# Announcing a loop's jump back in every pass except the last

## The chip, the cores and the metric

One core of a Trainium2 chip. The metric is the device time of one execution in microseconds (us), lower is better. Of each kernel several executions were timed and one was traced; "the trace" is that one.

## The reference

One decode step: layer norm of a single token, attention of 16 heads, each over its own cache of 65,536 keys and values of 256 numbers, an output projection, and a gated dense branch beside it. What matters is the cache: 1.07 GB of bf16 are read once.

```python
x = A_x
xn = _layernorm(x, axis=-1)
s = _A_ref(xn, A_k_cache, A_v_cache, A_wq, A_wo)   # scores, softmax, weighted values, @ wo
g = _silu(_B_ref(xn, B_w1, B_w2))
return x + s * g
```

## The kernel before

The cache is cut into 64 blocks of 8 MB of keys and 8 MB of values. Three buffers of 8 MB hold, in turn, the keys of a block and then the values of the same block. VectorE multiplies the keys with the query and sums most products, ScalarE sums the rest and makes the softmax, TensorE finds the row maximum and multiplies with the values, and SyncE's queue issues the transfers. Each engine has its own loop of three blocks a pass, synchronised by semaphores alone.

```python
    def load_k(i, s):
        take(sp, vf[s])                 # the values in this buffer are used up
        sp.dma_start(out=R[s][:, :], in_=block(Kd, i)).then_inc(kl[s], 16)
        sp.sem_inc(kh[s], 16)

    def load_v(i, s):
        take(sp, kf[s])                 # the keys in this buffer are used up
        sp.dma_start(out=R[s][:, :], in_=block(Vd, i)).then_inc(vl[s], 16)

    def pe_v(s):
        take(pe, pv)
        take(pe, vl[s], 16)
        pe_keys(psO, s, s, 0, KB, True, True, od)      # 64 matmuls
        pe_mark().then_inc(vf[s], 1)

    def pe_block(i, s):
        pe_turn()
        pe_max(i)
        pe_v(s)

    def loop(e, a, b, step, **kw):
        return nc.Fori(a, b, step, engines={e}, head_slot={e: 0}, **kw)
    # ... cut ...
        with loop(ET.DVE, 0, LAST - 2, NR, hint_back_edge=True) as i:
            for s in range(NR):
                dve_block(s)
    # ... cut: the same for ScalarE, and for TensorE from 1 to LAST - 4 ...
        pe_block(NBLK - 3, 0)           # after the loop: value block 60
        pe_turn()
        pe_v(1)
        pe_max(NBLK - 2)
    # ... cut ...
        dve_block(0, between=first_heads)   # after the loop: the last keys, in two halves
```

The option `hint_back_edge` puts one hint at the head of each pass: a record of 39 ns on VectorE in late passes, in the trace of before. By its name it announces the jump at the pass's end; what it does inside is not shown by any trace, only what leaving it out does (e8: VectorE then idles 6.1 to 6.8 us at each jump back).

## Time and profile before

| | before |
|---|---|
| time, median of 3 (lowest to highest) | 2526.43 us (2525.76 to 2526.54) |
| span of the trace | 2523.2 us |
| busy: VectorE, ScalarE, TensorE | 89%, 57%, 47% |
| data queue, share of 16 DMA engines' span | 99.5% |

The queue's row says what bounds the kernel. The engines' shares do not say where time is lost: two stalls of 5.5 us (TensorE) and 6.8 us (VectorE) near the end hide in them, each of which ends 1.4 to 1.5 us after an instruction packet has landed. The prediction shows and reads the lines for this. One pair of lines that it uses only in passing is needed below: TensorE near the end (start us, us, engine, line, operation, count, idle before and what ended it).

```profile
2506.12 0.36 PE L649 MATMUL bank<-hist,ones_sq 128*128 128x5 f32 x2
2507.47 3.61 PE L318 MATMUL bank<-R,PV 128*2 128x512 bf16 x16 [0.99 <-DMA R<-in_A_v_cache_dram]
```

The first line is the last step of VectorE's path: products of the last keys, row maximum, softmax, sums. It ends at 2506.48. The second line needs that *and* the third piece of the last value block, which lands at 2507.43. So two paths meet here, only 0.95 us apart.

### The profile page before, as it was taken

To read this page: it belongs to the slowest core of one execution; us is meant where nothing else is said; L and a number is where in the kernel's file an instruction comes from. 1 tells how busy PE (TensorE), PEld (TensorE's weight loads), DVE (VectorE), ACT (ScalarE), POOL (GpSimd) and SP (SyncE) were. 2 spreads that over 40 slices of the span, in tenths; PEclk is the share of its full clock that TensorE was granted. 3 is DMA by queue.
4 is the path that set the end of the run, shared out by engine and by line. 5 is a ranking of instruction groups with operands and counts; after the bars stand their busy time and mean duration, and the time that the engine had idled before them with its cause. 6 is when DMAs were issued, how large, how long until landed. Compare 5 with 4: busy or idle time off the path is not lost. (4 is left out here: it accounts for less than half of the span.)

```text
span 2523.2 us, 29918 instructions
## 1 busy us (share of the span) xinstructions
PE 1198.1 (47%) x5125; PEld 500.5 (20%) x5125; DVE 2233.7 (89%) x10281; ACT 1443.9 (57%) x6992; POOL 2.5 (0%) x13
## 2 busy tenths in 40 slices
PE   3353543534535435445354354454553543534556
PEld 2121211212212112112121121221221211212222
DVE  6989889889899898898898988988989889889886
ACT  3656556556555565565565655655656556556554
POOL 0000000000000000000000000000000000000000
PEclk7676767767767767677676676676766767767778
DMA  9999999999999999999999999999999999999998
GB/s 423 417 430 433 434 431 433 433 432 432 432 432 432 433 434 437 434 435 433 433 433 432 432 432 432 432 433 434 439 434 433 433 433 433 432 432 432 432 412 346
DMA packets 22728, 1084.52 MB, mean 430 GB/s; under 512 B 2354, under 2 KB 4532, under 8 KB 4916
## 3 DMA queue, kind: packets, MB, share of 16 engines
q1 hardware_dynamic: 22706, 1084.30, 99.5%
q8 instruction: 6, 0.10, 0.0%
q14 instruction: 14, 0.11, 0.0%
q10 hardware_dynamic: 2, 0.00, 0.0%
HBM read 1084.29 MB, written 0.00 MB: 430 GB/s over the span
## 5 line engine op out<-in xcount | busy, mean ns | idle before, releaser
L271 ACT ACTIVATE R<-R 128x256 bf16<-128x256 bf16 x3328 | 1330.7, 401 | 697.1 <-ACTq L154 697.1
L249 DVE CUSTOM_DVE_ANT_0 R<-R,qcur 128x256 bf16<-128x256 bf16 x4864 | 1700.2, 417 | 0.0
L318 PE MATMUL bank<-R,PV 128*2 128x512 bf16 x4096 | 1023.7, 416 | 32.4 <-DMA R<-in_A_v_cache_dram 15.3
L238 DVE TENSOR_TENSOR R<-R,qcur 128x3328 bf16<-128x3328 bf16 x256 | 482.6, 1885 | 198.7 <-DVEq L154 198.6
L271 ACT ACTIVATION_READ_ACCUMULATOR R<-R 128x1 f32 x3328 | 620.2, 186 | 2.6 <-issue 2.6
L330 PE MATMUL bank<-ident,rmax 128*1 128x128 bf16 x65 | 17.1, 263 | 1021.6 <-PEq L154 1021.6
L318 PEld LDWEIGHTS bank<-R,PV 128*2 128x2 bf16 x4096 | 365.0, 90 | 663.1 <-issue 208.0
L249 DVE DVE_READ_ACCUMULATOR2_ANT S<- 128x1 f32 x4864 | 383.5, 79 | 0.0
L346 PE MATMUL bank<-eye,O 2*128 2x1 f32 x536 | 98.0, 300 | 236.8 <-PEq L154 236.8
L330 PEld LDWEIGHTS bank<-ident,rmax 128*1 128x1 bf16 x65 | 5.2, 79 | 1026.1 <-issue 1025.9
L346 PEld LDWEIGHTS bank<-eye,O 2*128 2x128 f32 x536 | 94.2, 257 | 254.8 <-issue 254.8
L284 ACT ACTIVATE hist<-bank 128x1 f32 (+1 forms) x65 | 11.1, 171 | 203.4 <-ACTq L154 203.4
L305 ACT COPY hist<-bank 128x2 f32 (+1 forms) x66 | 10.5, 160 | 120.0 <-ACTq L154 120.0
L214 DVE TENSOR_REDUCE gmax<-bank 1x1 bf16<-1x128 f32 x65 | 18.2, 281 | 36.2 <-DVEq L154 36.2
L231 DVE CAST qcur<-bank 128x256 bf16<-128x256 f32 x64 | 27.2, 425 | 20.2 <-DVEq L154 18.3
L297 ACT COPY O<-bank 2x512 f32<-2x512 f32 x67 | 37.5, 559 | 9.1 <-ACTq L154 9.1
L286 ACT ACTIVATE PV<-S,hist 128x128 bf16<-128x128 f32 (+1 forms) x65 | 26.0, 400 | 13.4 <-ACTq L154 13.1
L358 PE MATMUL bank<-q,ident 16*128 16x256 bf16 x63 | 24.4, 387 | 0.0
L224 DVE COPY S<-S 128x128 f32<-128x128 f32 (+1 forms) x65 | 14.7, 226 | 9.5
L225 DVE TENSOR_REDUCE rmax<-S 128x1 bf16<-128x128 f32 (+1 forms) x65 | 18.2, 279 | 0.0
L336 PE MATMUL bank<-gmax,ones_row 1*128 1x1 bf16 x65 | 10.3, 158 | 15.9 <-PEq L154 15.9
L336 PEld LDWEIGHTS bank<-gmax,ones_row 1*128 1x128 bf16 x65 | 6.5, 99 | 33.3 <-issue 33.3
(65 smaller groups left out, 101.7 us busy)
## 6 DMA issues: line engine op xcount, KB each, us to landing
R<-in_A_k_cache_dram SPq DMA_DIRECT2D x4, 4096.0 KB, 23.4
R<-in_A_v_cache_dram SPq DMA_DIRECT2D x7, 2048.0 KB, 23.1
R<-in_A_wq_dram SPq DMA_DIRECT2D x1, 3072.0 KB, 12.7
R<-in_A_wo_dram SPq DMA_DIRECT2D x2, 1120.0 KB, 17.5
R<-in_B_w_dram SPq DMA_DIRECT2D x1, 1568.0 KB, 27.2
R<-in_B_w_dram SPq DMA_DIRECT2D x1, 1344.0 KB, 5.8
R<-in_A_v_cache_dram SPq DMA_DIRECT2D x1, 1024.0 KB, 15.8
R<-in_A_v_cache_dram SPq DMA_DIRECT2D x2, 512.0 KB, 17.0
```

Source lines behind the costliest of these rows:

```text
L214: dve.reduce_max(out=gmax[0:1, :], in_=ps_m[0:1, :], axis=AX.X).then_inc(gm, 1)
L225: dve.reduce_max(out=rmax[:, :], in_=S[:, c0:c1], axis=AX.X).then_inc(rm, 1)
L231: dve.tensor_copy(out=qcur[:, :], in_=ps_q).then_inc(sd, 1)
L238: m = dve.tensor_tensor(out=pair, in0=pair, in1=qcur[:, None, :].to_broadcast([P, NA, Dh]), op=ALU.mult,)
L249: ins = dve.tensor_tensor_reduce(out=Kv[:, c, :], in0=Kv[:, c, :], in1=qcur[:, :], scale=1.0, scalar=0.0, op0=ALU.mult, op1=ALU.add, accum ...
L271: ins = act.activation(out=prod, in_=prod, func=ACT.Identity, accum_out=S[:, c : c + 1],)
L286: act.activation(out=PV[s][:, c0:c1], in_=S2[:, c0:c1], func=ACT.Exp, bias=col(0, 1), scale=scale, accum_out=col(1, 2),).then_inc(pv, 1)
L297: act.copy(out=O[:, :], in_=po).then_inc(oc, 1)
L318: ins = pe.matmul(po, lhsT=PV[t][:, c : c + 2], rhs=R[s][:, c * Dh : (c + 2) * Dh], start=(start and c == k0), stop=(stop and c == k1 - 2),)
L330: pe.matmul(ps_m[0:1, :], lhsT=rmax[:, 0:1], rhs=ident[:, :], start=True, stop=True).then_inc(tm, 1)
L346: ins = pe.matmul(ps_t[:, a : a + 1], lhsT=Ov[:, j, a, :], rhs=eye2[:, j : j + 1], start=(j == 0), stop=(j == 1),)
L358: pe.matmul(ps_q, lhsT=ident[0:H, at(h)].to_broadcast([H, P]), rhs=q16[:, :], start=True, stop=True,).then_inc(qr, 1)
```

## The change

The intent: in the last pass the jump back is not taken, and in the trace of before the code after the loop came late, by the two stalls above. My guess was that the hint in the last pass is the reason, and that without it the code after the loop is there in time.

```diff
+    @contextmanager
+    def loop(g, a, b, step):
+        es, name = {g.engine}, f"passes_{nc.next_id()}"
+        head, ann, body, tail = (f"{name}_{x}" for x in ("head", "ann", "body", "tail"))
+        # ... cut: register, addr_align with offset=0 ...
+        with nc.body(head, valid_engines=es):
+            g.br_eq(r, b - step, on_true=body, on_false=ann)
+        with nc.body(ann, valid_engines=es):
+            hint = g.mark_branch_hint_location()
+            nc.br(body, engines=es)
+        with nc.body(body, valid_engines=es):
+            yield nc.snap(r, min_val=a, max_val=b - step)
+            nc.regs_alu(r, r, step, op=mybir.AluOpType.add)
+            g.br_lt(r, b, on_true=head, on_false=tail).branch_hint(hint)
+        nc.switch_bb(tail)
-        with loop(ET.DVE, 0, LAST - 2, NR, hint_back_edge=True) as i:
+        with loop(dve, 0, LAST, NR) as i:
```

ScalarE's and TensorE's loops change alike. SyncE's loop stays as it was, without hints.

## The prediction

61 and 223 ns are the compare-and-branch that closes a loop's pass, and the "0.1 to 0.4 us" a pass are an estimate from these and from the 275 ns. "Prefetch in sequence" is my reading of one 16 KB packet, which landed at 2432.88 us with no stall after it: the trace gives a packet's time and size, not what is in it. The "25 us or more" and "about 5 us for a fetch" of rival 2 are estimates too, and 433 GB/s is 992.62 MB in the 2290 us from 120 to 2410.

> **What bounds the kernel now.** I read the page's slices and queues first, to see which resource is never free.
>
> ```profile
> DVE  6989889889899898898898988988989889889886
> DMA  9999999999999999999999999999999999999998
> q1 hardware_dynamic: 22706, 1084.30, 99.5%
> ```
>
> The second row, in tenths of 16 DMA engines, is full from the first slice to the last but one; VectorE's row is 8 to 9. The data queue took 99.5% of 16 engines' span. So the key and value caches' transfer sets the pace: 1084.3 MB at 430 GB/s. A wait on a compute engine costs time only if it makes the queue run dry, or if it lies after the last transfer that matters.
>
> Second, the chain that ended last, in order of time (start us, us, what), for the end:
>
> ```profile
> 2484.34 23.09 DMA R<-in_A_v_cache_dram
> 2507.43 0.04 issue
> 2507.47 3.61 PE bank L318 x16
> ```
>
> The last link that waits is the third piece of the last value block (2 MB). From its landing at 2507.43 us to the span's end at 2523.2 there are 15.8 us of TensorE, two VectorE additions and the output. So the end is "DMA stream, plus 15.8 us".
>
> Third, the groups with their idle time, restricted to the steady stretch from 120 to 2410 us:
>
> ```profile
> L238 DVE TENSOR_TENSOR R<-R,qcur 128x3328 bf16<-128x3328 bf16 x237 | 446.8, 1885 | 189.3 <-DVEq L154 189.3
> ```
>
> Once a block (59 blocks) VectorE stands idle before its first product for 189.3 / 59 = 3.2 us; in the code that wait is for the key block's landing. VectorE is nearly full, but it is the DMA's follower.
>
> Fourth, the list of waits from 2380 us on, for what happens where the loops end:
>
> ```profile
> DVE qcur L231 <- DVEq L154: 6.8, 1, 6.8
> ...
> PE bank L318 <- issue: 5.5, 1, 5.5
> ...
> ACT R L271 <- issue: 2.6, 1, 2.6
> ```
>
> Three single waits. "issue" means that nothing which the profile shows was awaited. VectorE's is the first instruction after its loop: its closing compare-and-branch starts at 2458.66, and its sequencer's next record is at 2465.50, though the query it needs was made on TensorE by 2458.62.
>
> Fifth, the DMA queues, first of the steady stretch 120 to 2410 us, then of 2410 to the end:
>
> ```profile
> q1 hardware_dynamic: 17034, 992.62, 100.2%
> ```
>
> ```profile
> q1 hardware_dynamic: 4072, 41.81, 87.6%
> q8 instruction: 4, 0.07, 0.2%
> q14 instruction: 5, 0.04, 0.1%
> ```
>
> In the steady passes no instruction is fetched at all[...]. Where the loops end, nine fetches appear. From the packet records: a 16 KB fetch on q8 lands at 2425.71 us, and TensorE resumes at 2427.17; an 8 KB fetch on q14 lands at 2464.07, and VectorE resumes at 2465.50. These three waits are instruction fetches[...].
>
> [...] after TensorE's missed block at 2425.71 the following block comes at 2432.88 without a stall at its boundary, so unhinted prefetch in sequence is seen working. [...] the trace has 61 ns on VectorE in late passes (223 ns on TensorE), and 275 ns from a taken one to the hint at the loop's head.
>
> **The change, part by part.** The loops' bounds are written differently, but the passes are the same: VectorE and ScalarE run 0 to 60 in steps of 3 (21), TensorE 1 to 58 (20). The compiled order shows no other move: each of three engines gets a compare-and-branch ahead of its hint and at most one unconditional branch behind it. The transfer queue's own loop is as before.
>
> *Added per pass.* On VectorE about 0.1 us, at most 0.4 if the unconditional branch is kept and costs what a taken one does. It stands at the head of a pass, ahead of the 3.2 us wait for keys, which absorbs it. ScalarE waits for VectorE's product there (3 to 4 us a time), and TensorE stands idle 16 us for the row maxima in each block. Sum on the path over 20 passes: 0.
>
> *Removed: the stall on VectorE.* 6.8 us at 2458.7. What does it delay? The first half of the last key block, which frees the buffer for the next transfers (issued at 2483.34). They would be issued near 2476.5. But by then 8 MB of keys and 12 MB of values are queued: the keys' packets start near 2443.5, and 20 MB (20.97 million bytes) at 433 GB/s take 48 us, to about 2492. The queue would not have been empty before 2492, so issuing at 2483 or at 2476 is the same. Worth 0. It also gives more slack to the last softmax, which ends just 1 us before the transfer that ends the chain.
>
> *Removed: the stall on ScalarE.* 2.6 us at 2471, in the sums of the same block. Worth 0 for the same reason.
>
> *Removed: the stall on TensorE.* This one reaches the queue. Its lines (start us, us, engine, line):
>
> ```profile
> 2420.18 1.44 PE L318 MATMUL bank<-R,PV 128*2 128x512 bf16 x3
> 2427.17 15.35 PE L318 MATMUL bank<-R,PV 128*2 128x512 bf16 x61 [5.55 <-issue]
> 2442.35 0.17 PE L368 MATMUL bank<-ident 128*1 128x1 bf16 x1
> ```
>
> Value block 60 is cut after three matmuls. Its end frees buffer 0 for the last key block, and the SyncE queue issues it at once:
>
> ```profile
> 2398.40 0.33 SPq L192 DMA_DIRECT2D R<-in_A_k_cache_dram  x1
> 2418.84 0.33 SPq L197 DMA_DIRECT2D R<-in_A_v_cache_dram  x1
> 2442.65 0.82 SPq L201 DMA_DIRECT2D R<-in_A_k_cache_dram  x2
> ```
>
> Issues normally come 18 to 21 us apart, against 8,388,608 B / 433 GB/s = 19.4 us for a block, with some 5 us queued. Here 23.8 us pass and the queue runs dry. From the packet records (start plus duration): engines begin to fall idle at 2441.0, the last at 2443.5, and all 16 are busy again at 2444.5. The idle time of 16 engines between 2440 and 2448, averaged, is 2.15 us; elsewhere between 2395 and 2510 it is none. Without the stall value block 60 ends at 2420.18 + 16.65 (block 59 took that uncut) = 2436.8; the keys are issued near 2437.1, some 4 us before the queue would empty. The gap closes whole.
>
> After that nothing should open another: the next values are issued at 2457.5, when VectorE finishes a block that it started before; the keys then run to about 2461. All transfers move up 2.15 us, and the 15.8 us after the third value piece stay.
>
> *Sum:* 2526.43 - 2.15 + 0 + 0 + 0 = 2524.3 us, 0.09% less.
>
> **The rivals.**
> 1. *The stalls count in full:* 5.5 + 6.8 = 12.3 us off, 2514. For it: both are real and stand one after the other. Against it: the queue is busy through the second, and was dry for 2.15 us after the first.
> 2. *Nothing is fetched ahead in the last pass either:* the stalls stay, 2526.4. For it: the trace holds no unhinted pass of these bodies, so that leaving a hint out restores sequential prefetch is inferred. Against it: the sequential fetch at 2432.88, and some 25 us or more between entering the loop's last block and its exit, against about 5 us for a fetch. I give it 15%.
> 3. *The added branches lie on the path:* 21 passes by 0.1 to 0.4 us = 2 to 8 us, 2528 to 2533. For it: VectorE is 89% busy. Against it: 3.2 us idle in each block behind the DMA. 4%.
> 4. *A new gap opens:* with buffer 0 refilled early, the queue holds just some 3 us when the next values are issued; if value block 61 or the row maxima came late, part of the 2.15 us would come back, 2525 to 2526. 6%.
>
> **Range and chances.** The mechanism gives 2524.3, the main rival 2526.4; three runs of before lie within 0.8 us, and another chip may shift both by some microseconds. Range 2521.5 to 2528.0. A 2% change is 50 us, more than all the waits named here together: faster 0.01, same 0.985, slower 0.005.
>
> **What would show it.** Right: the waits of 6.8 us (VectorE's query copy) and 5.5 us (TensorE, "issue") gone or under 1 us; value block 60 in one piece of 64 matmuls; the last keys issued near 2437; no idle DMA time near 2442; instruction fetches some tens of microseconds before the loops' ends; the chain still ending through the third value piece, near 2505.3; the span near 2521.0. Wrong: stalls at the same places (rival 2), a longer period of the passes than 38.8 us a block (rival 3), a DMA gap after 2457 (rival 4), or a chain that no longer goes through the DMA (rival 1).

## The result, and the profile after

| | before | after |
|---|---|---|
| time, median (lowest to highest) | 2526.1 us (2524.6 to 2526.54), 4 runs | 2523.24 us (2522.64 to 2524.02), 4 runs |
| span of the trace | 2523.2 us | 2520.7 us |

The ratio is 0.999, with a 95% interval from 0.9973 to 1.0007. Here and below the ratio and its interval are from fast runs compared round by round, so not quite the ratio of the medians. By the 2% measure the two are the same. The ranges do not overlap, though, and they did not in a second measurement either (e1 below). The gain is 2.9 us by the medians and 2.5 us by the traces.

The page's rows after, the answers to those shown of before:

```profile
DVE  6989889889898898898898988988989889889897
DMA  9999999999999999999999999999999999999998
q1 hardware_dynamic: 22706, 1084.30, 99.6%
```

The bound is the same. In the list of waits from 2380 us on, VectorE's wait after its loop is down to 0.9 us, and the lines of 5.5 us (TensorE) and 2.6 us (ScalarE) are gone:

```profile
DVE qcur L231 <- DVEq L154: 0.9, 1, 0.9
```

TensorE's value block 60, in one piece, and the transfers that SyncE issued around it:

```profile
2420.40 16.05 PE L318 MATMUL bank<-R,PV 128*2 128x512 bf16 x64
2436.29 0.17 PE L368 MATMUL bank<-ident 128*1 128x1 bf16 x1
```

```profile
2396.55 0.33 SPq L192 DMA_DIRECT2D R<-in_A_k_cache_dram  x1
2419.06 0.33 SPq L197 DMA_DIRECT2D R<-in_A_v_cache_dram  x1
2436.58 0.82 SPq L201 DMA_DIRECT2D R<-in_A_k_cache_dram  x2
```

The last keys go out at 2436.58 instead of 2442.65. From the packet records the 16 DMA engines have no idle time between 2438 and 2449 us, where they had 2.14 us. The DMA queues between 2300 and 2410 us show the fetch that is now made ahead (a 16 KB packet, at 2351.4 us by its record):

```profile
q8 instruction: 1, 0.02, 0.1%
```

The end of the chain of what ended last:

```profile
2479.93 24.97 DMA R<-in_A_v_cache_dram
2504.91 0.04 issue
2504.95 3.61 PE bank L318 x16
```

The third value piece lands at 2504.91, 2.52 us earlier than before; from the next matmul to the end the two chains have the same pieces.

### The profile page after: what moved, and what is told of

Its sections match the earlier page's. It is cut to its first block, busy times and chain, and to the rows that moved or that the text cites. A ratio compares the mean times of both kernels' runs of the same rounds, so it can differ in the third digit from the quotient of the medians.

```text
span 2520.7 us, 29977 instructions
## 1 busy us (share of the span) xinstructions
PE 1198.9 (48%) x5125; PEld 500.4 (20%) x5125; DVE 2233.5 (89%) x10281; ACT 1443.8 (57%) x6992; POOL 2.5 (0%) x13
## 6 DMA issues: line engine op xcount, KB each, us to landing
R<-in_A_v_cache_dram SPq DMA_DIRECT2D x1, 1024.0 KB, 15.7
```

## The experiments

Theory at the start: all of the gain comes from TensorE's stall, by the DMA gap. Rivals: VectorE's stall is part of it; or the new layout of the code is the cause, not the omitted hint. All runs gave right results, with five executions each (e10: six), e1 to e4 on one chip and e5 to e12 on another. The kernel before took 2525.95 us in the median on the first (2524.98 to 2528.42) and 2527.46 to 2527.83 on the second (2525.16 to 2530.12). So the second chip's runs are compared with each other and with its own runs of before; e9 to e12 came in a later batch, in which only one further run of before was made.

### e1: the changed kernel again

No edit.

> The changed kernel, unaltered, for a second measurement on this chip. If the gain is real: 2.2 to 3.4 us below the kernel before in the same rounds, with an interval that excludes zero, and no idle time of the DMA engines between 2395 and 2505 us. If it was chance between few runs: within 1 us of the kernel before.

Measured: 2523.01 us (2522.93 to 2524.37), ratio 0.9989 (0.9976 to 1.0003). The mean is 2.7 us below that of before, without overlap. The interval misses excluding zero by a hair, so that part of the expectation failed; no DMA engine idles between 2395 and 2505. In this trace the two paths meet even closer: the third value piece lands at 2505.25, the sums that end VectorE's path run from 2504.96 to 2505.32, and the next matmul starts at 2505.29.

### e2: TensorE's loop alone

```diff
-        with loop(dve, 0, LAST, NR) as i:
+        with nc.Fori(0, LAST - 2, NR, engines={ET.DVE}, head_slot={ET.DVE: 0}, hint_back_edge=True) as i:
```

ScalarE's loop likewise.

> Only TensorE's loop omits the hint in its last pass; VectorE's and ScalarE's loops are as before. My theory (TensorE's stall delays the last keys' issue and the DMA queue runs dry): the whole gain, 2.2 to 3.2 us below before, with VectorE's stall of some 6.8 us still in the trace. Rival (VectorE's stall, which holds up the start of the last block, is part of the gain): less than half of it, 0 to 1.2 us.

Measured: 2527.94 us (2524.7 to 2528.79), ratio 1.0007 (0.9993 to 1.0021). No gain. In the trace TensorE's stall and the DMA gap are gone, as in the changed kernel, and VectorE's stall of 6.3 us is there. The chain now begins elsewhere:

```profile
2506.51 0.36 PE bank L668 x2
2506.86 3.54 PE bank L318 x16
```

L668 is the sum that ends VectorE's path (L649 before). TensorE waited for its row maximum, which it had not needed to in the changed kernel:

```profile
2504.05 0.22 PE L330 MATMUL bank<-ident,rmax 128*1 128x128 bf16 x1 [1.33 <-PEq L154]
```

So my theory falls in its first form. The DMA path moved up (the value piece is not waited for any more), but VectorE's path stayed, and the matmuls behind both could start just 0.6 us earlier than before (2506.86 in this list, against 2507.47). The trace, 0.6 us shorter than that of before, is of the fastest of the five executions; the slower ones have no trace, so why the mean lies 1.2 us *above* before stays open.

### e3: VectorE's and ScalarE's loops alone

```diff
-        with loop(pe, 1, LAST - 2, NR) as i:
+        with nc.Fori(1, LAST - 4, NR, engines={ET.PE}, head_slot={ET.PE: 0}, hint_back_edge=True) as i:
```

> Only VectorE's and ScalarE's loops omit the hint in the last pass; TensorE's is as before. My theory: no gain, within 0.7 us of before, with TensorE's stall of about 5.5 us and a DMA gap of about 2 us near 2442 still there, though VectorE's 6.8 us are gone. Rival (VectorE's stall is part of the gain): 1 to 3 us below before.

Measured: 2526.53 us (2523.37 to 2526.67), ratio 0.9998 (0.9985 to 1.0012): no gain that stands out. In the list of waits TensorE's stall is as before, VectorE's is gone, and the chain begins with the DMA at the old time:

```profile
PE bank L318 <- issue: 5.8, 1, 5.8
...
DVE qcur L231 <- DVEq L154: 0.9, 1, 0.9
```

```profile
2479.23 28.20 DMA R<-in_A_v_cache_dram
```

It lands at 2507.43. The DMA engines idle for 1.48 us. Together, e1, e2 and e3 say that either half alone brings nothing clear, and both bring 2.7 us. (e12 below is a second run of e3's kind, with a ratio of 0.9994, so this half may bring some tenths of a microsecond to 1.5 us.) The reading: two paths of nearly the same length end together, and each stall lies on one of them.

### e4: the new loop, with the hint in all passes

```diff
-            g.br_eq(r, b - step, on_true=body, on_false=ann)
+            g.br_eq(r, b, on_true=body, on_false=ann)
```

> The changed loops with the same added branches, but the test at the head never holds, so that the hint is given in the last pass too. My theory (it is the omission that matters, not the layout or the branches): both stalls are back (5 to 7 us each) and the time is that of before, within 0.7 us. Rival (the new layout of the code brings the gain): the time of the changed kernel, 2.2 us or more below before.

Measured: 2526.44 us (2525.01 to 2528.09), ratio 0.9999 (0.9986 to 1.0013), the time of before. So the new layout and branches alone do not bring the gain. But TensorE's stall is not back, only VectorE's, 6.0 us, and ScalarE's, 2.5 us. TensorE had none in value block 60 (64 matmuls in one piece, 16.67 us); its packet came at 2405.50 by the packet record, in an idle wait. The two-path reading fits (VectorE's path ends the chain, as in e2). That TensorE needed no omission here was a surprise, taken up in e12: for TensorE alone, this run does not separate the omitted hint from the new layout.

### e5, e9, e10: a delay on TensorE without a fetch

The changed kernel, with 13, 25 and 37 idle matmuls ahead of value block 60.

```diff
-        pe_block(NBLK - 3, 0)
+        pe_turn()
+        pe_max(NBLK - 3)
+        for _ in range(13):        # 25, 37
+            pe.matmul(
+                psO, lhsT=ident[:, 0:2], rhs=ident[:, 0:1].to_broadcast([P, 2 * Dh]),
+                start=True, stop=True,
+            )
+        pe_v(0)
```

> The changed kernel with 13 idle matmuls of some 0.43 us ahead of value block 60 on TensorE: the delay of before (5.5 us) without any missing instruction. My theory: the last keys are issued near 2442 again, the DMA gap is back (1.5 to 2.5 us idle), and the time is 1.5 to 2.8 us above the changed kernel, so near before. Rival (a fetch costs time in another way than by the delay, for example on the DMA queues): within 0.7 us of the changed kernel.

Measured: 2523.55 us (2523.18 to 2526.55), as fast as the changed kernel. The experiment missed its dose. These are its lines for the idle matmuls and for value block 60:

```profile
2420.95 5.29 PE L612 MATMUL bank<-ident 128*2 128x512 bf16 x13
2426.08 13.97 PE L318 MATMUL bank<-R,PV 128*2 128x512 bf16 x64
```

They took 5.3 us, but value block 60 then took 13.97 us instead of about 16, and the keys went out at 2440.18, just before the queue would have run dry (0.02 us of idle time). The granted clock explains it: in the trace of before, the weight loads of these matmuls start 0.427 us apart while it is 0.50 and 0.216 us apart once it is 1.00 (at 2431.30 us). In the changed kernel value block 60 starts at 2420.40 with a granted clock of 0.50, which goes to 1.00 at 2424.64 us, 4.2 us after steady matmuls began. In e5 it goes to 1.00 at 2425.68 us, 4.7 us after the idle matmuls began, and value block 60 starts only at 2426.08. So it took 13.97 us / 64 = 0.218 us a matmul here, and 16.05 / 64 = 0.251 there. So the dose was raised:

> The changed kernel with 25 idle matmuls ahead of value block 60. With 13 the last keys were issued at 2440.2, just before the queue would empty, because the matmuls also warmed the clock, so that value block 60 ran faster; 12 more at 0.214 us add 2.6 us. Two-path theory: keys issued near 2442.7, 1.5 to 2.5 us of idle DMA, the end 1.5 to 2.5 us above the changed kernel though VectorE has no stall. Rival (the DMA gap does not set the end): within 0.7 us of the changed kernel.

> The same with 37 idle matmuls, 12 more, 2.6 us more. Two-path theory: once the queue is dry each microsecond of later issue is one of later end: keys near 2445.3, 4 to 5 us of idle DMA, 4 to 5 us above the changed kernel. Rival: no rise from 25 to 37 idle matmuls.

Measured: 25 matmuls 2526.74 us (2525.35 to 2528.88), 37 matmuls 2528.0 us (2527.16 to 2530.82). With the other runs of that chip in which VectorE has no stall that matters:

| run | DMA idle, 2438 to 2449 us of the trace | mean time |
|---|---|---|
| e7 (below) | none | 2523.89 |
| e11 (below) | none | 2524.17 |
| e5, 13 idle matmuls | 0.02 us | 2524.23 |
| e12 (below), stall of 6.2 us | 1.56 us | 2525.38 |
| e9, 25 idle matmuls | 1.40 us | 2526.70 |
| e10, 37 idle matmuls | 3.70 us | 2528.39 |

From e5 to e10 the queue idles 3.7 us longer and the mean time rises by 4.2 us. Not all of that rise is the queue's, though. By the traces the third value piece lands 3.07 us later in e10 than in e5 (2508.52 against 2505.45), and the matmuls behind it then take 5.30 us instead of 3.61, while the granted clock is 0.50 from 2509.42 to 2512.83 us, where e5 had 1.00:

```profile
2508.57 5.30 PE bank L318 x16
```

e9's trace has the same 5.30 us; it is also of the slowest of its five executions, and its transfers were some 3 us behind e5's already at 2430 us, before any gap. So a late issue of the last keys without a fetch delays the last transfers by about what the queue stands empty; that is shown by e5 and e10, and e9 adds little to it.

### e6, e11: a delay on VectorE without a fetch

The changed kernel, with eight and three reciprocals before VectorE's last block.

```diff
+        for _ in range(8):         # 3
+            t_d = mark("dve", dve.reciprocal(
+                out=part[:, :, :].rearrange("p a e -> p (a e)")[:, 0:P], in_=ones_sq[:, :]
+            ))
+            need("dve", t_d)
         dve_block(0, between=first_heads)
```

> The changed kernel with eight reciprocals of 128 columns, some 6.8 us by the rate of the row for 448 columns (2.94 us), on VectorE between its loop and its last block: the delay of before without any missing instruction. My theory: it lies beside the DMA stream, within 0.7 us of the changed kernel. Rival (the start of VectorE's last block is on the path): 2 us or more above the changed kernel.

Measured: 2529.83 us (2527.48 to 2531.32), mean 2529.50; above all runs in the table, and 2.2 us above the mean of before. My expectation was wrong, the rival's right. The delay, on VectorE, and the start of the chain:

```profile
2460.99 7.86 DVE L697 RECIPROCAL part<-ones_sq 128x128 f32<-128x128 f32 x8 [0.76 <-issue]
```

```profile
2509.50 0.36 PE bank L668 x2
```

VectorE's last block starts at 2468.99 here, and its path's last step 40.51 us after that. The distance is the same 40.51 us in before (2465.61 to 2506.12) and in e2 (2466.00 to 2506.51). The third value piece lands at 2504.86 here and at 2505.21 in e2. So VectorE's block may start until about 2464.5 before its path becomes the end. In the changed kernel's trace it starts at 2461.21, which leaves some 3.3 us of room, an estimate from these numbers; the delay of 7.9 us is more. (In that trace the last step comes 1.2 us later than 40.51 us after the start, since TensorE is still busy with work on an earlier value piece; that is harmless, as it stays ahead of the transfer.)

> The changed kernel with three reciprocals (0.98 us each as measured, 2.9 us in all) on VectorE ahead of its last block, instead of eight (7.9 us, which cost some 5 us). Two-path theory: VectorE's path has some 3 to 4 us of room behind the DMA stream in the changed kernel, so this costs nothing, within 0.8 us of the changed kernel. Rival (VectorE's path is the bound in the changed kernel): about 2.9 us above it.

Measured: 2523.59 us (2523.14 to 2525.96), mean 2524.17, 0.3 us above e7: inside the room, as expected. The block starts at 2464.59, the last step comes 40.51 us later, at 2505.10, and ends at 2505.46; the value piece lands at 2505.41. The room is just used up.

### e7: no hint at all on TensorE

```diff
-        with loop(pe, 1, LAST - 2, NR) as i:
+        with nc.Fori(1, LAST - 4, NR, engines={ET.PE}, head_slot={ET.PE: 0}) as i:
```

> TensorE's loop with no hint in any pass, as a plain loop; the other two as changed. By my theory fetching goes on in sequence when there is no hint, so the exit is smooth and the last keys go out near 2437; each jump back may then stall TensorE's sequencer 3 to 6 us, but it stands ahead of a wait for ScalarE and an idle time of 16 us, so that costs nothing: within 0.7 us of the changed kernel. Rival (the hint is needed in each pass): 20 passes by 2 us or more of dry queue, 40 us or more above.

Measured: 2524.05 us (2522.99 to 2525.06), mean 3.4 us below before. Right in the time, but with less than I expected: there is no stall at the jumps back, and no fetch on TensorE's queue (q8) between 143 and 2424 us. One extra 16 KB fetch is recorded at 143.03 us, in the first pass, and the list of waits from 2380 us on has no stall of TensorE at the loop's end. So that packet may have brought the code after the loop, to be used 2.3 ms later; what is in a packet the trace does not show. TensorE needed neither the hint nor its omission here.

### e8: no hint at all on VectorE

```diff
-        with loop(dve, 0, LAST, NR) as i:
+        with nc.Fori(0, LAST - 2, NR, engines={ET.DVE}, head_slot={ET.DVE: 0}) as i:
```

> VectorE's loop with no hint in any pass; the other two as changed. My theory: a stall of 5 to 7 us at each jump back, 3.2 us of which lie in the wait for keys that follows; the rest delays one value issue in three by 2 to 4 us, less than the 5 us that stand in the queue: within 1.5 us of the changed kernel. Rival (VectorE at 89% has no room for it): 20 passes by 2 to 4 us, 40 to 80 us above.

Measured: 2626.49 us (2625.43 to 2628.85), ratio 1.0396. I expected nothing, the rival 40 to 80 us; it was 100. The waits of VectorE (us in total, times, longest):

```profile
DVE qcur L231 <- DVEq L154: 133.8, 22, 6.8
```

At each jump back VectorE stands idle for 6.1 to 6.8 us. The DMA queues of one pass (1227 to 1348 us):

```profile
q1 hardware_dynamic: 863, 50.27, 98.1%
q14 instruction: 5, 0.04, 0.1%
```

Five packets of 8 KB are fetched in this pass, and 115 in the whole run against 14 in e1; a pass of the changed kernel (1181 to 1297 us) has none. A pass grows from 116.1 to 121.2 us, and the DMA engines idle in it for 2.5 us. So VectorE's 3.2 us of waiting for keys are no room to spend. From the code: the keys' buffer is freed by values that were issued only when VectorE had finished an earlier block, so a late VectorE makes its own keys late. The trace has a sign of it: the wait for keys falls from 2.9 us to nothing in a pass's first block, but rises from 3.2 to 4.2 us in the two others. The cause is still argued and not tested, and the idle time is but half of the growth.

### e12: TensorE's old loop, begun four slots later

Like e3, with one more difference:

```diff
-head_slot={ET.PE: 0}
+head_slot={ET.PE: 4}
```

> TensorE's loop as before the change, hint in every pass, but begun at slot 4 of a fetch block instead of 0; VectorE and ScalarE as changed. My explanation of the run with the hint in all passes, where TensorE's stall was missing[...]. So here no stall in value block 60, the keys issued near 2437, and the time of the changed kernel within 0.8 us. If the explanation is wrong: the stall of 5 to 6 us is there, only some two matmuls earlier, and the time is 2 to 3 us above.

Measured: 2524.79 us (2523.84 to 2528.01), mean 1.2 us above e11 and 1.9 us below before on this chip, so the time fits neither expectation. The stall is there, two matmuls earlier:

```profile
2420.67 0.58 PE L318 MATMUL bank<-R,PV 128*2 128x512 bf16 x1
2427.41 15.15 PE L318 MATMUL bank<-R,PV 128*2 128x512 bf16 x63 [6.16 <-issue]
```

So my explanation of e4 was wrong. It named the point in the code at which the next fetch is asked for, a guess that no run shows, and concluded that a loop begun some slots later has no stall. What the run does show is that the place of the stall depends on the slot at which the loop begins: four slots later, the block is cut after one matmul instead of three (before and e3). Each matmul has a weight load of its own (5125 of each on the page of before), so two matmuls are four instructions. Why e4 fetched early stays open.

One sum over the traces puts the two paths together. Take the later of the two: the landing of the third value piece, or the end of the sums on VectorE's path. From there to the span's end it is 15.7 to 15.8 us in ten traces (before, after, e1, e2, e3, e5, e6, e7, e11, e12). It is longer in e4 (16.2), e9 and e10 (17.5), where the 16 matmuls that follow took 4.03 us (e4) and 5.30 us (e9, e10) instead of 3.54 to 3.61; in e10 the granted clock was 0.50 for 3.4 us there. So whichever path is later sets the end.

## Why the prediction was right

**The sum and its landmarks were right.** 2524.3 us was predicted, 2523.24 measured. The last keys were to go out near 2437.1 (2436.58), the gap to close (closed), the third value piece to land near 2505.3 (2504.91), the span to be 2521.0 (2520.7). The piece came up 2.52 us instead of 2.15; the remaining 0.37 us is less than the spread of the runs, and I do not explain it. Three small slips in the working change nothing: a block takes 116.11 / 3 = 38.7 us and not 38.8, the last DMA engine fell idle at 2443.1 and not 2443.5, and rival 3's 2528 to 2533 mixes a sum with the gap's 2.15 us taken off and one without.

**The prefetch without a hint was right.** With the hint omitted in the last pass the fetches come in time: a 16 KB packet on TensorE's queue at 2351.4, and two packets of 8 KB on the queue of VectorE and ScalarE (q14) at 2431.5 and 2434.4, more than 25 us ahead of these two loops' exits (2460.2 and 2461.3); the stalls of 5.5 and 2.6 us are gone and VectorE's wait of 6.8 is down to 0.9. In e2, where these two loops keep the hint, those two packets are missing. Rival 2 is out. For TensorE the omission is one way among several: with the new loop and the hint in all passes (e4), or with no hint at all (e7), it had no stall in value block 60 either. The stalls of before (5.5 us on TensorE, 6.8 us on VectorE) follow jumps that are not taken; a stall at a taken jump is the one of e8 (6.1 to 6.8 us).

**The added branches cost nothing: right.** VectorE's wait for keys in the first block of a pass fell from 3.00 to 2.91 us, which is the 0.09 us from the new branch to the hint; the period is 116.11 us in both traces. In late passes of the changed kernel a compare-and-branch that is not taken occupied 50 ns on VectorE and 75 ns on TensorE, one that is taken 74 and 221 ns. Rival 3 is out.

**The step that failed** is the term "Removed: the stall on VectorE. ... Worth 0", and with it the reading that TensorE's 2.15 us could be booked alone. I followed what that stall delays only as far as the transfers, which were indeed queued anyway. Its other follower is the last softmax. I wrote that it ends "just 1 us before the transfer that ends the chain" and did not draw the consequence: the DMA path can come up by at most about 1 us before VectorE's path becomes the end. By the traces TensorE's part alone was worth 0.6 us (e2), VectorE's alone nothing in e3 and 0.7 in e12, the two together 2.5. The total came out right because the change did both, so to that extent by luck: the 2.15 us were booked to one stall, and needed the removal of the other.

**Absorption** was used too freely: the wait of 3.2 us did take up 0.09 us, but it does not take up 6.1 to 6.8 us a pass (e8).

**Rival 4** came half true without harm: the row maximum of block 62 came 1.5 us late (2460.06 against 2458.56), and no gap opened.

## What to carry to other kernels

When two paths meet close together, note the distance between them before pricing a wait: taking a stall off the longer one is worth no more than that distance, until the other is shortened too. A stall that looks harmless beside a full queue must be followed to every consumer, not to the transfers alone. And leaving the hint for a loop's jump back out of the last pass alone was right for VectorE here, where leaving it out of all passes cost 100 us; on TensorE a plain loop did as well. The whole gain is 0.1% of the time, near the noise.
